# The input loaded already transposed, instead of transposed on TensorE

## The chip, the cores and the metric

The kernel runs on one core of a Trainium2 chip. A core has five engines that work side by side, each in the order of its own instruction stream: TensorE (PE, matrix products), VectorE (DVE), ScalarE (ACT), GpSimd (POOL) and SyncE (SP, which here only issues transfers). They wait for each other by semaphores. Transfers between the main memory and the core's on-chip memory (SBUF) run on 16 DMA engines that all queues share. TensorE reads SBUF and writes PSUM, an accumulator memory of eight banks; DVE and ACT read PSUM back. The metric is the device time of one execution in microseconds (us).

## What is computed

Two attentions over the same input `x` (2048 positions by 640, bf16), with 32 heads of 20 dimensions each, are mixed by a gate. From the reference:

```
g = sigmoid((x * gate_w).sum(-1))
a = A(x, A_wqkv, A_wo)   # softmax(q k^T * 20**-0.5) v for every head, then @ wo
b = B(x, B_wqkv, B_wo)   # each position sees itself and 7 earlier ones, 2 apart
out = g * a + (1 - g) * b
```

A is the costly part: 32 heads by 2048 by 2048 scores, each of which needs an exponential.

## The kernel before, in words

All work is written as tasks by `T(engine, function, reads, writes)`. A planner (`_Sched`) keeps the tasks of an engine in the order in which they are written and derives the semaphore waits from the named buffers. So the order of the source lines is the order on each engine, and SP issues its transfers in that order too.

*The main part.* Heads are taken four at a time (a "quad"), queries 512 at a time. A step computes the scores of two or three pairs (head, block of 128 keys) on PE (line 1241) into PSUM banks 0 to 2 or 3 and 4, and ACT takes the exponential of all of them in one instruction (line 1256). PE multiplies the results with the values (line 1281). 777 such exponentials follow each other. Two fifths of the score blocks go to DVE instead, by an arithmetic exponential (lines 1424 to 1448). The local attention B and the output products are woven between by a list of lanes with due times, planned when the program is built.

*The prologue*, which is all that the change touches, prepares what the first step needs. PE's products contract over the partition dimension, so the input must stand with its 640 features on partitions: `xT[128, 4, 5, 512]`, four stretches of 512 positions, five blocks of 128 features. In order:

- `WqkA` receives the key weights of the first quad by ACT's queue (line 383) and its query weights by SP's (line 388). Between them SP issues eight loads of 256 positions each into `x_tm`, position on partitions (line 385). Behind them on SP come the gate vector `gw` (line 392, 640 single elements) and the value weights `WvA` (line 395).
- `pe_warm` (line 408) issues seven matmuls on zeros while the transfers are on their way.
- `pro_tr(h)` transposes load `h` on PE: ten 128 by 128 blocks, in a group of six and one of four, into PSUM (line 1112). DVE copies the first group to `xT` (line 1124), ACT the second (line 1121).
- `pro_k(h)` computes the keys of the first quad for these 256 positions (five matmuls, line 1136). DVE takes the largest absolute key (line 1140), and ACT then copies the keys to `kT` (line 1142). The transposes and the keys of the eight loads alternate on PE.
- `mk_KM` makes from these maxima a matrix `KM` on DVE (lines 490 and 494), which bounds the scores. `pro_q` computes the first 512 queries (line 1153), DVE takes their absolute value (`q_abs`, line 659), and `q_fin` adds on PE the bound, that is the product of `KM` and that absolute value (line 664), and scales the result on DVE to `qT` (line 667).
- The first three blocks of values (`v_chunk`, 15 matmuls, line 565) are evacuated by ACT (lines 586 and 594). Their weights need the gate vector as a column: a DVE copy into `WvA` (line 1183).
- Two filler matmuls (`pe_fill`, line 1199), and then the first step's scores and its exponential.

On PE the order at the end of the prologue is: the two halves of the first queries, the values, the bound's product, the filler, the first scores. On SP, behind `WvA`, come the key and query weights of the next quads (`ld_wk`, `ld_wq`, line 441, five transfers of 20 KB each, in runs of 40 bytes), the value weights of B (line 674) and, from 48 us on, the other weights of B (`WqkB`, line 888, in runs of 256 bytes).

## Time and profile before

| | us |
|---|---|
| median of 3 runs (894.79 to 896.25) | 895.59 |
| the profiled execution | 894.33 |
| its span in the profile | 892.5 |
| busy: ACT | 876.2 |
| busy: PE | 820.1 |
| busy: DVE | 811.9 |
| busy: POOL | 87.8 |
| first exponential starts at | 18.18 |

The span runs from the first to the last instruction of the profiled execution; what the execution takes beyond it, 1.83 us, lies around it. Times in the views are counted from the span's start. A group of instructions is named by its line, engine and operation, then by what it writes and reads; "idle before" is how long the engine had stood still, and "<-" names what ended that. The profile names a buffer by its memory, so `oTn`, `accW` and `qk` can stand for other buffers that share the place: `accW` in the prologue is the key weights' tile `WkP`.

### The profile page before, as it was taken

Reading aid. Unit: us, or ns where it says so; the run is one execution under the profiler, and the core shown is the slowest. Engines: PE = TensorE matmul, PEld = TensorE weight load, DVE = VectorE, ACT = ScalarE, POOL = GpSimd, SP = SyncE. Lnnn points to the kernel's source line nnn. Section 1 sums busy time; section 2 is a strip of 40 time slices with the busy share of each in tenths; the row PEclk is TensorE's granted clock in tenths of the full one; section 3 lists DMA queues with packets and bytes.
Section 4 is the critical chain, followed back from the end, with each engine's and each line's share of the span. In section 5 each row is a group of like instructions: output and inputs, shape, how many; then the busy total and the mean of one; then the engine's idle time right before and its main releaser. Section 6 shows DMA issues by size and latency. Waiting matters only on the chain.

```text
span 892.5 us, 15877 instructions
## 1 busy us (share of the span) xinstructions
PE 820.1 (92%) x6560; PEld 255.5 (29%) x6560; DVE 811.9 (91%) x1170; ACT 876.2 (98%) x804; POOL 87.8 (10%) x103
## 2 busy tenths in 40 slices
PE   9989999999999998999998889999988999888986
PEld 6322322223323222223332222233222232222322
DVE  6598889999998999999899999999999899999994
ACT  6999999999999999999999999999999999999996
POOL 1000000000000011220002222001322002222000
PEclk9999999999999999999999999999999999999999
DMA  8122101011011456572115658113847003865000
GB/s 181 41 49 48 21 9 10 1 28 7 4 11 14 86 93 94 90 123 37 17 19 88 111 102 145 25 16 56 143 78 108 10 10 74 131 93 89 2 1 30
DMA packets 140988, 51.26 MB, mean 57 GB/s; under 512 B 120436, under 2 KB 128628, under 8 KB 140916
## 3 DMA queue, kind: packets, MB, share of 16 engines
q0 software_dynamic: 13824, 31.46, 20.5%
q1 hardware_dynamic: 126164, 18.35, 13.4%
q8 instruction: 52, 0.85, 0.4%
q10 hardware_dynamic: 928, 0.43, 0.2%
q14 instruction: 20, 0.16, 0.1%
HBM read 16.14 MB, written 2.62 MB: 21 GB/s over the span
## 4 chain that ended last, share of the span: by engine, by line
ACT 94%; PE 2%; DMA 2%; DVE 1%; issue 0%; POOL 0%; DVEq 0%
ACT ebuf L1256 93%; DMA accW<-tmps 1%; PE ps L1112 1%; DMA accW<-xT 1%; PE ps L1136 1%; ACT L_sb L1004 0%; PE ps L411 0%; PE ps L1241 0%; DVE tmps L1069 0%; DVE accW L1059 0%; DVE qk L905 0%; ACT WvB L841 0%; PE ps L565 0%; DVE xH L1436 0%; PE ps L1153 0%
## 5 line engine op out<-in xcount | busy, mean ns | idle before, releaser
L1256 ACT ACTIVATE ebuf<-ps 128x1024 bf16<-128x1024 f32 (+1 forms) x777 | 862.7, 1485 | 0.9 <-PE ps L1241 0.8
L1241 PE MATMUL ps<-qT,kT 32*128 32x512 bf16 x1941 | 305.6, 384 | 63.9 <-ACT ebuf L1256 55.1
L1281 PE MATMUL ps<-ebuf,vA 128*21 128x512 bf16 x1902 | 182.6, 383 | 0.5 <-ACT ebuf L1256 0.5
L1241 PEld LDWEIGHTS ps<-qT,kT 32*128 32x128 bf16 x1941 | 74.3, 91 | 351.7 <-ACT ebuf L1256 327.2
L1424 DVE TENSOR_SCALAR xI<-ps 128x512 int32<-128x512 f32 x146 | 99.4, 686 | 28.3 <-PE ps L1396 14.8
L1436 DVE SCALAR_TENSOR_TENSOR xH<-xU 128x1024 f32<-128x1024 f32 x73 | 88.9, 1218 | 1.4
L1071 POOL DMA_DIRECT2D accW<-tmps x36 | 32.0, 987 | 586.2 <-DVE tmps L1069 545.8
L1439 DVE SCALAR_TENSOR_TENSOR xH<-xH,xU 128x1024 f32<-128x1024 f32 x73 | 88.7, 1216 | 1.0
L1448 DVE SCALAR_TENSOR_TENSOR xo<-xI,xH 128x1024 int16<-128x1024 int32 x73 | 88.7, 1215 | 0.6
L463 PE MATMUL ps<-xT,WqkB 128*128 128x512 bf16 x200 | 59.9, 383 | 0.0
L1281 PEld LDWEIGHTS ps<-ebuf,vA 128*21 128x21 bf16 x1902 | 35.8, 90 | 64.6 <-issue 56.7
L942 DVE TENSOR_TENSOR prod<-qk 128x1024 bf16<-128x1024 bf16 x80 | 51.8, 681 | 0.3 <-PE ps L918 0.3
L1433 DVE TENSOR_SCALAR xU<-xI 128x1024 f32<-128x1024 uint16 x73 | 49.8, 682 | 0.6
L463 PE MATMUL ps<-xT,WqP 128*128 128x512 bf16 x155 | 46.7, 383 | 0.0
L463 PE MATMUL ps<-woA_r,oTn 128*128 128x320 bf16 x236 | 45.3, 301 | 0.0
L463 PE MATMUL ps<-xT,accW 128*128 128x512 bf16 x140 | 42.2, 383 | 0.0
L1717 PE MATMUL ps<-ident,zt 128*128 128x512 bf16 x119 | 40.8, 386 | 0.0
L1712 PE MATMUL ps<-xT,ident 128*128 128x512 bf16 x130 | 40.1, 384 | 0.6 <-DVE qk L905 0.6
L1396 PE MATMUL ps<-qT,kT 32*128 32x512 bf16 x107 | 38.9, 383 | 0.8 <-DVE kT L475 0.7
L1069 DVE TENSOR_TENSOR tmps<-vB,attnT 128x1280 f32<-128x1280 bf16 x24 | 35.5, 1478 | 1.4 <-DMA accW<-tmps 1.4
L1069 DVE TENSOR_TENSOR xT<-vB,attnT 128x1280 f32<-128x1280 bf16 x24 | 35.4, 1477 | 0.3 <-DMA xT<-xT 0.3
L463 PE MATMUL ps<-WvA,oBacc 128*128 128x320 bf16 x160 | 33.2, 302 | 0.1
(122 smaller groups left out, 730.1 us busy)
## 6 DMA issues: line engine op xcount, KB each, us to landing
accW<-tmps POOLq DMA_DIRECT2D x36, 320.0 KB, 4.2
accW<-xT POOLq DMA_DIRECT2D x24, 320.0 KB, 4.0
xT<-xT POOLq DMA_DIRECT2D x24, 320.0 KB, 4.6
WqkB<-in_B_wqkv_dram SPq DMA_DIRECT2D x40, 160.0 KB
xT<-tmps POOLq DMA_DIRECT2D x12, 320.0 KB, 3.8
WqP<-in_A_wqkv_dram SPq DMA_DIRECT2D x135, 20.0 KB
x_tm<-in_A_x_dram SPq DMA_DIRECT2D x8, 320.0 KB
out_dram<-outsb SPq DMA_DIRECT2D x24, 80.0 KB
```

The source lines that it names most:

```text
L463: ins = e.matmul(o, l, r, start=(k0 + k == 0), stop=(k0 + k == n - 1))
L942: t = T("dve", lambda e, r=r, q_ap=q_ap, k_ap=k_ap: e.tensor_tensor(prod[r][:, :, :], q_ap, k_ap, ALU.mult), reads=["qB", "kB"], writes=[( ...
L1069: T("dve", lambda e, vv=vv, av=av, m=m: e.tensor_tensor(tmp4[m], vv, av, ALU.mult), reads=["aT", "vB4"], writes=[("tmps", m)] + dead, cost ...
L1241: ins = e.matmul(bank[b0 + i], kT[32 * j:32 * j + 32, q, kb * P:(kb + 1) * P], qT[gi % NQT][32 * j:32 * j + 32, :], start=True, stop=True)
L1256: return T("act", lambda e: e.activation(ebuf[s % NEB][:, 0:512 * n], ps[:, b0 * 512:(b0 + n) * 512], ACTF.Exp, scale=LN2 / ONE), reads=[( ...
L1281: ins = e.matmul(bank[OB][32 * j:32 * j + DH + 1, :], vA[:, q, kb, VW * j:VW * j + DH + 1], ap, start=st, stop=sp)
L1424: r = T("dve", lambda e, b=b, i=i: e.tensor_scalar(xI[:, 512 * i:512 * i + 512].bitcast(I32), bank[b], XB, 0.0, op0=ALU.add, op1=ALU.max), ...
L1433: T("dve", lambda e: e.tensor_scalar(xU[:, :], xI[:, :].bitcast(U16)[:, 0:2048:2], XV[0], XV[1], op0=ALU.mult, op1=ALU.add), reads=[("xI", ...
L1436: T("dve", lambda e: e.scalar_tensor_tensor(xH[:, :], xU[:, :], XC[0], xU[:, :], ALU.add, ALU.mult), reads=["xU"], writes=["xH"], cost=1220)
L1439: T("dve", lambda e: e.scalar_tensor_tensor(xH[:, :], xH[:, :], XC[1], xU[:, :], ALU.add, ALU.mult), reads=["xU"], writes=["xH"], cost=1220)
L1448: t = T("dve", lambda e, r=r: e.scalar_tensor_tensor(xo[r][:, :].bitcast(I16), xI[:, :].bitcast(I32), XC[2], xH[:, :], ALU.mult, ALU.add), ...
L1717: T("pe", lambda e: e.matmul(bank[OB], zt[:, :], ones4, start=False, stop=False, skip_group_check=True), reads=["ident", "zt"], accum=[("o ...
```

## The change

The eight loads of the input become transposing transfers that write `xT` directly. PE's transposes and the DVE and ACT copies that followed them are left out. The load of the first query weights is issued after the fourth of the eight instead of after the eighth. The keys of the eight loads follow each other on PE. The two halves of the first queries come behind the keys of loads 5 and 6 (counted from 0), and behind the keys of the other six stands a single filler matmul (`pe_idle`). The bound's product, with its scaling to `qT`, is written ahead of the gate vector's copy and of the first values; the values stand directly before the filler. The further weights of the next quad are issued behind the fourth key product in the source, which leaves their place on SP's queue.

```
-        T("sp", lambda e, h=h: e.dma_start(x_tm[:, 2 * h:2 * h + 2, :], x_v[:, 2 * h:2 * h + 2, :]),
-          writes=[("x_tm", h)], dma=True)
-
-    T("sp", lambda e: e.dma_start(WqkA[:, :, 0:80], wA_v[:, :, 0:80]), writes=[("WqA", 0)], dma=True)
+        T("sp", lambda e, h=h: e.dma_start_transpose(xT[:, h // 2, :, 256 * (h % 2):256 * (h % 2) + 256], A_x[0][256 * h:256 * h + 256, :]),
+          writes=[("xTt", h)], dma=True)
+        if h == 3:
+            T("sp", lambda e: e.dma_start(WqkA[:, :, 0:80], wA_v[:, :, 0:80]), writes=[("WqA", 0)], dma=True)
...
+    sch.bufs[("bk", 0)] = [sch.bufs[("bk", 7)][0], []]
...
-    def pro_tr(h):
...
-            T("pe", pe_tr, reads=[("x_tm", h), "ident"], writes=[("bk", b)])
...
-        T("pe", fn, reads=w_keys("WkP", 0) + [("xTt", h, k) for k in range(2)], writes=[("bk", b)], cost=550)
+        T("pe", fn, reads=w_keys("WkP", 0) + [("xTt", h)], writes=[("bk", b)], cost=550)
...
-    pro_tr(0)
-    pro_tr(1)
-    pro_k(0)
...
+    def pe_idle(n):
+
+        def fn(e):
+            ins = None
+            for _ in range(n):
+                ins = e.matmul(bank[0], zt[:, :], fap(zt, zt[:, 0:1], [[0, 4], [1, P]]), start=True, stop=True)
+            return ins
+
+        T("pe", fn, reads=["zt"], accum=[("bk", 0)])
+
+    for h in range(NH):
+        pro_k(h)
+        if h == 3:
             ld_wk(1)
             ld_wq(1)
-    pro_tr(NH - 1)
-    for h in range(NH - 3, NH):
-        pro_k(h)
-        if h == NH - 3:
+        if h == 4:
             mk_q0()
+        if h in (5, 6):
+            pro_q(h - 5)
+        else:
+            pe_idle(1)
     mk_KM(0, 0)
     mk_KM(0, 1)
-    pro_q(0)
+    q_fin(QB0, 0, 0)
     T("dve", lambda e: e.tensor_copy(WvA[:, :, 1:2], gw[:, :].rearrange("p (c k) -> p c k", k=1)), reads=["gw", "WvA"],
       writes=["WvA"], cost=170)
-    pro_q(1)
...
     for i_ in range(3):
         v_chunk(3, 0, 0, i_, i_)
     v_evac(3, 0, 0, "act")
-    q_fin(QB0, 0, 0)
```

30 lines of the change are left out of this document (2 added, 28 removed).

## The prediction

> **What bounds the kernel now.** I read the page's parts 1, 4 and 5 first, to see which engine sets the time.
>
> ```profile
> span 892.5 us, 15877 instructions
> ...
> PE 820.1 (92%) x6560; PEld 255.5 (29%) x6560; DVE 811.9 (91%) x1170; ACT 876.2 (98%) x804; POOL 87.8 (10%) x103
> ...
> ACT 94%; PE 2%; DMA 2%; DVE 1%; issue 0%; POOL 0%; DVEq 0%
> ...
> L1256 ACT ACTIVATE ebuf<-ps 128x1024 bf16<-128x1024 f32 (+1 forms) x777 | 862.7, 1485 | 0.9 <-PE ps L1241 0.8
> ```
>
> The 777 exponentials run on ACT with 0.9 us of idle time in all, 0.8 of it before the first. So the time is the start of the first exponential, a fixed 862.7 us, and the tail. The change lies wholly ahead of the first exponential; what it moves that start by, it moves the end by. The second view is the chain of waits for the first 20 us (start, length, what), which shows what sets that start.
>
> ```profile
> 0.99 3.17 PE ps L411 x7
> 4.16 2.11 PE ps L1112 x20
> ...
> 12.56 1.74 PE ps L1136 x15
> 14.29 1.09 PE ps L1153 x10
> 15.39 0.03 issue
> 15.41 1.23 PE ps L565 x15
> 16.65 0.24 PE ps L664
> 16.89 0.02 issue
> 16.91 0.70 DVE qT L667
> 17.61 0.14 issue
> 17.75 0.41 PE ps L1241 x3
> 18.16 0.02 issue
> 18.18 2.37 ACT ebuf L1256 x2
> ```
>
> PE carries it from 4.16 to 16.89: transposes (L1112), first keys (L1136), first queries (L1153), values (L565), bound's product (L664). The first exponential starts at 18.18. Third, the transfers of the same 20 us, 40 slices of 0.5 us (busy tenths, then rate):
>
> ```profile
> DMA  0005699999999999999999899999623539567747
> GB/s 0 0 0 54 95 323 303 339 397 341 356 374 364 369 364 369 371 361 366 323 198 206 195 310 351 365 235 104 45 12 21 31 21 56 33 38 45 55 30 46
> ```
>
> Summed by slice, 2.73 MB have passed at 10.0 us: the input (2.62 MB, rows of 1280 B) and the 0.10 MB of key weights. The full rate is 366 GB/s, so the input takes 7.16 us. The slow stretch after it holds the query weights and the gate vector; the value weights (WvA, 0.82 MB) end at about 13.45. So the transfers end well before the PE chain needs them. Fourth, the only transfers with the new load's run length: WqkB is read in runs of 256 B, in slices of 0.075 us from 49.5 us.
>
> ```profile
> DMA  7531144889766758999999999999999989642100
> GB/s 44 27 43 27 32 56 96 191 198 236 181 150 140 157 126 181 225 239 277 266 263 253 253 253 287 280 256 277 270 205 229 222 188 201 127 85 48 21 14 17
> ```
>
> With the engines at 9 tenths it holds 253 to 287 GB/s; the middle of the band, less its edges, is about 259.
>
> **The change part by part.**
>
> *Taken out.* PE's 80 transposes (the first 20 matmuls take 2.11 us in the chain, later groups of ten 0.56 each, 5.5 in all), eight DVE copies of 0.55 us, eight ACT copies of 0.59 us. All of it is gone from PE's path. Next late is the DMA.
>
> *The load.* Each of the eight now reads 256 rows by five column blocks, that is 1280 runs of 256 B. No transposing transfer is in this trace. Ends: not under 7.16 us for all eight, the copy rate (the bytes are the same); the slow end is the nearest row of smaller pieces, the key weights' runs of 40 B, at some 36 GB/s from 14 us on: 73 us. I take the row with the same run length, 259 GB/s: 2.621 MB / 259 = 10.12 us, 2.96 more. The ramp at the start (1.5 to 3 us) is kept. So the input ends at 12.96 instead of 10.0, and WvA, which stays behind it on SP's queue, at 16.4 instead of 13.45.
>
> The Trainium skill, "DMA: Bandwidth & Descriptors", § Latency and other measured facts, gives 261 GB/s for a transposing transfer with a non-contiguous middle dimension; by it the load would take 10.04 us and the sum below would be 0.1 us less.
>
> *Issue on SP.* The eight input issues took 0.47 us each; WqkB's 640 runs take 0.37 to issue, so 1280 runs 0.74 us; eight are 5.9 us, under the 10.1 us that the data take: nothing. The other end is WvA, 640 runs in 2.04 us, but those come while its queue is full: 4.1 us for 1280, 33 us for eight. I take 0.74, the row with these runs. The query weights' issue (0.52 us) goes between the fourth and the fifth; the same bytes pass ahead of WvA either way. Later on the queue, the next key weights slip by the same 3 us; they land some 8 us ahead of their first use at 28.3, so nothing.
>
> *The key chain.* From the last load's landing t7 (12.96): product to reduction 0.75 (6.11 to 6.86 in this trace), reduction to the bound KM 0.94 (14.34 to 15.28), bound's product and its scaling to qT 1.13 (16.48 to 17.61), some 0.15 of handovers: qT is there at t7 + 3.0 = 15.96. The first queries' two products and |q| on DVE (0.69) come two loads earlier, between arrivals 1.26 us apart: nothing.
>
> *The bound's product ahead of the values.* The gate column's copy into WvA (0.17, L1183) now stands behind qT on DVE, and the value products wait for that copy. So qT does not overlap the values: with the input free, that order costs. Before, KM's end at 15.28 led to an exponential at 18.18, 2.90. After: 0.05 + 1.13 + 0.05, then 0.22 from copy to values, then 2.0 to the exponential, 3.45. But WvA's landing (16.4) is later than qT (15.96), and so the move costs nothing here. Without WvA's wait it would cost 0.5.
>
> *Values to exponential.* In this trace value products start at 15.41, and ACT has finished their two evacuations at 17.38: 1.97. On PE: 1.07 of values, 0.43 of filler, three score products 0.41 to 0.43: 1.95 to 2.05. Both say 2.0.
>
> *Added.* Six single filler matmuls between keys, about 0.22 us each of issue: in the gaps between arrivals. The one behind the eighth key product lies beside the reduction (0.42): nothing.
>
> *Sum.* 16.4 + 0.05 + 0.22 + 2.0 = 18.67, against 18.18: **+0.5 us**. The profiled execution took 894.33 (span 892.5, 1.83 around it), which gives 894.8; the median shown is 1.26 above the profiled one, so 896.1. The point at which the change turns from gain to loss is an input time of 9.6 us, 272 GB/s: inside the band of WqkB's rates. 0.2% (1.8 us) is about what a measurement of this kernel can tell from no change.
>
> **The rivals.**
>
> *A, the copy rate: faster.* The transposing load keeps 366 GB/s, whatever the runs are, as if whole rows of 1280 B were still fetched. WvA then lands at 13.45 and the exponential starts at 15.72: -2.46, 893.1; at 330 GB/s -1.7, 893.9. For it: the same queue does 366 in this trace. Against it: WqkB's runs never pass 287. It passes 0.2% from 335 GB/s up.
>
> The Trainium skill, "Advanced Engine Details and Errata", § X-Bar Transpose (TRN2), says transposing transfers are as fast as regular ones and expects 350 to 400 GB/s; no run here shows one.
>
> *B, a fixed part in each transposing transfer: slower.* Eight loads stream without a gap before. If each transposing one must drain before the next begins, each pays something of its own start. The nearest row is the ramp, from first bytes at 1.5 to the full rate, worth 1.03 us of full-rate data: seven more of it are 7.2 us, 903.3. It decides from 0.16 us per load (+1.3 on top of the forecast, 897.4). For it: 100 KB of key weights took 3.5 us from issue to landing, though their bytes are worth 0.3 us, so a transfer that must be whole is dear. Against it: nothing here shows that transfers of one queue wait for each other. Its middle is 900.
>
> *C, the PE clock.* The seven warming matmuls of L411 are 0.425 us apart, and filler of the same width later 0.215: half speed until about 4.3 us. The granted clock of the profile reads 1.00 there too, so spacing is what shows it. PE was full after that; now it works some 1.1 of the 3.4 us ahead of the values. If it falls back to half speed there, values and filler take 1.5 us more, the first scores 0.2, and the next 3.3 us, with PE 92% busy, lose 1.3: +3.0, 899.1. Against it: no gap before WvA is longer than some 1.5 us.
>
> The Trainium skill, "TensorE: Matmul & The Clock Gate", § HAM oscillation — how this bites in real kernels, warns of idle gaps over 3.4 us, which by it would leave this kernel at the forecast.
>
> *D, the load broken into small pieces*, each at the price of the key weights' 40 B runs: 73 us instead of 10.1, 959. For it: turning rows into columns scatters what was one run. Against it: nothing in this trace.
>
> The Trainium skill, "VectorE: DVE Perf Modes", § The three transpose paths, gives 1309 ns for one 128 by 128 block by DMA against 390 on TensorE; 80 blocks one after another would by an estimate from that page take 105 us, and no run here shows it.
>
> **How the numbers follow.** Forecast (230 to 290 GB/s, its own range 895.0 to 897.4) 0.32: no change 0.29, slower 0.03. A 0.24: faster 0.21, no change 0.03. B 0.27, C 0.12, D 0.05: slower. So faster 0.21, same 0.32, slower 0.47; the likeliest single case is the forecast, 896.1, though slower has more in sum. The range goes from A's end, 892.9, to B's, 903.5, and leaves out D, B's far part and a little below A, some 0.14.
>
> **What would show it.** In the changed kernel's profile: no L1112 or L1124 rows; input transfers at about 260 GB/s until 13; key products about 1.26 us apart, each waiting for a DMA; the gate copy (L1183's) waiting for WvA's DMA, not for qT; the first exponential near 18.7. A is right if the rate is over 320 and the exponential starts before 16.8; B if the transfers' busy tenths dip between loads; C if the value products (68 ns apart now) are about 134 apart. The forecast is wrong if SP's issues are over 1.3 us each, so that the sequencer paces the load, or if ACT waits between later exponentials by more than now.

## The result, and the profile after

The changed kernel takes 904.7 us in the median of four runs (903.27 to 907.04), against 895.71 for the kernel before beside it (894.79 to 896.25): a ratio of 1.0104, 95% interval 1.0081 to 1.0127. It is slower by 9.0 us. The profiled execution took 903.27, its span 901.4, so 8.9 us more on each than before.

The page of the changed kernel first: span, the shares of the chain, the exponentials.

```profile
span 901.4 us, 15624 instructions
...
ACT 88%; DVE 5%; DMA 3%; SPq 2%; PE 2%; issue 1%; POOL 0%; DVEq 0%
...
L1236 ACT ACTIVATE ebuf<-ps 128x1024 bf16<-128x1024 f32 (+1 forms) x777 | 863.0, 1473 | 2.4 <-PE ps L1221 2.4
```

ACT still sets the time, and its work is the same: 863.0 us against 862.7. Its waits went from 0.9 to 2.4 us, of which 0.7 lies ahead of the first exponential (before: 0.8). (The description of the kernel before gives two fifths of the score blocks to DVE; the page has 146 of the 32 × 16 × 4 = 2048, on line 1424 before and 1404 after, so ACT has 93% of them.) The rest of the 8.9 us is ahead of ACT's main part, in the chain of waits of the first 40 us (start, length, what).

```profile
0.74 1.38 SPq L385
...
13.12 1.84 SPq L385
...
15.00 0.58 SPq L392
...
15.62 5.78 DMA WvA<-in_A_wqkv_dram
...
21.49 0.19 DVE WvA L1165
...
21.73 2.06 PE ps L566 x15
23.79 0.85 PE ps L1179 x2
24.64 0.57 PE ps L1221 x2
...
25.23 15.02 ACT ebuf L1236 x13
```

SP's issues (L385 are the eight input loads) carry the chain until 15.6, then the landing of the value weights, then PE. The first exponential starts at 25.23 instead of 18.18. The accounts, both from profiled executions:

| us | before | after | difference |
|---|---|---|---|
| first exponential starts | 18.18 | 25.23 | +7.05 |
| exponentials, busy | 862.7 | 863.0 | +0.3 |
| waits between later exponentials | 0.1 | 1.7 | +1.6 |
| sum | | | +8.95 (span: +8.9) |

The transfers of the first 20 us, 40 slices of 0.5 us (busy tenths, then rate), answer to the view that the load was priced from:

```profile
DMA  0000999989979967994698999979999793379999
GB/s 0 0 0 15 183 220 266 205 161 113 286 170 179 288 152 154 230 239 83 126 160 172 283 210 183 273 138 109 200 271 182 137 259 8 32 139 284 369 387 366
```

The rate reaches 260 to 290 GB/s again and again and falls to 80 to 150 in between. The input ends at 17.3 instead of 12.96, and the plain copy of WvA behind it runs at 366 to 387. The stretches around the wait for WvA (from:to, length, busy time and count of PE, weight loads, DVE, ACT, POOL, then granted PE clock, DMA share, GB/s):

```profile
20.00:21.00 1.00, 0.00 (x0) 0.00 (x0) 0.20 (x1) 0.00 (x0) 0.00 (x0) 1.00 1.36 108
21.00:22.00 1.00, 0.27 (x4) 0.28 (x5) 0.40 (x2) 0.00 (x0) 0.00 (x0) 0.96 0.47 28
22.00:23.00 1.00, 1.00 (x10) 1.00 (x8) 0.87 (x4) 0.00 (x0) 0.00 (x0) 0.50 0.61 37
```

The clock falls to 0.50 just as the value products begin, and the chain above shows them at 2.06 us, where the chain of before has 1.23. PE had stood from 18.3 to 21.7 but for the bound's product (its weights load at 19.1; the record of its matmul is missing).

So of the 6.56 us by which the first exponential missed the forecast's 18.67, 5.0 are the landing of WvA (21.4 for 16.4) and 1.5 the half clock from the values on.

### The profile page after: what moved, and what is told of

The parts are those of the page before. It is cut to its first block, busy times and chain, and to the rows that moved or that the text cites. A ratio compares the mean times of both kernels' runs of the same rounds, so it can differ in the third digit from the quotient of the medians.

```text
span 901.4 us, 15624 instructions
## 1 busy us (share of the span) xinstructions
PE 803.3 (89%) x6399; PEld 251.3 (28%) x6486; DVE 807.7 (90%) x1162; ACT 872.4 (97%) x796; POOL 87.8 (10%) x103
## 4 chain that ended last, share of the span: by engine, by line
ACT 88%; DVE 5%; DMA 3%; SPq 2%; PE 2%; issue 1%; POOL 0%; DVEq 0%
ACT ebuf L1236 87%; DMA xT<-xT 1%; SPq L385 1%; DVE prod L943 1%; DVE xT L1070 1%; DMA WvA<-in_A_wqkv_dram 1%; DVE xo L1428 1%; DMA accW<-tmps 1%; DVE xI L1404 0%; PE ps L1221 0%; ACT L_sb L1005 0%; PE ps L1692 0%; DVE xH L1419 0%; PE ps L1261 0%; DVE xH L1416 0%
## 5 line engine op out<-in xcount | busy, mean ns | idle before, releaser
L1236 ACT ACTIVATE ebuf<-ps 128x1024 bf16<-128x1024 f32 (+1 forms) x777 | 863.0, 1473 | 2.4 <-PE ps L1221 2.4
L464 PE MATMUL ps<-xT,WqkB 128*128 128x512 bf16 x179 | 53.3, 383 | 1.8 <-issue 1.6
L464 PE MATMUL ps<-xT,WqP 128*128 128x512 bf16 x136 | 41.5, 383 | 1.5 <-issue 1.1
L464 PE MATMUL ps<-xT,accW 128*128 128x512 bf16 x126 | 38.1, 383 | 1.6 <-issue 1.4
L1692 PE MATMUL ps<-xT,ident 128*128 128x512 bf16 x113 | 35.8, 387 | 3.9 <-DVE xI L1404 1.8
L566 PE MATMUL ps<-WvA,xT 128*128 128x160 bf16 (+1 forms) x320 | 31.0, 238 | 3.5 <-DVE WvA L1165 3.5
```

The source lines that it names most:

```text
L464: ins = e.matmul(o, l, r, start=(k0 + k == 0), stop=(k0 + k == n - 1))
L1236: return T("act", lambda e: e.activation(ebuf[s % NEB][:, 0:512 * n], ps[:, b0 * 512:(b0 + n) * 512], ACTF.Exp, scale=LN2 / ONE), reads=[( ...
```

## The experiments

Three questions were open. First, why the load is slow: "issue" says that SP's sequencer paces it, "stream" that the transposing transfers are slow in the DMA engines and SP only waits for room; later "runs" blames the 256 B runs, "mixing" the plain transfers among transposing ones, "boundary" the change from one transposing transfer to the next, "size" the small piece. Second, whether the late start passes to the end. Third, what the half clock and the new order cost. The kernel before took 895.3 to 895.7 in the median beside each of them.

**probe_sizes.** The transfers alone, each waited for before the next, then groups back to back.

```
+ e.dma_start_transpose(xT[:, 0, :, :], x[0:256, :])   # waited for; then other shapes
+ for h in range(8): e.dma_start_transpose(xT[:, h, :, :], x[256*h:256*h+256, :])
...
+ for c in range(5): e.dma_start(xR[:, :, :, c, :], x_v[:, :, c*P:(c+1)*P])   # runs of 256 B
```

> A program of transfers alone, all issued from SP; it leaves out the whole computation, and what it writes out is the input. First, transposing loads one at a time, each waited for before the next is issued (256 by 640 twice, 128 by 640, 64 by 640, 512 by 640, 1024 by 640, 256 by 256, 256 by 128, 128 by 128), then one plain load of 256 by 640 and one of its first 128 columns; then eight transposing loads of 256 by 640 back to back, four of 512 by 640, eight plain ones, and the same bytes in runs of 256 B. Theory 'issue' (SP makes the pieces of a transposing load one by one, and this paces the eight): with the queue empty the 256 by 640 load still takes 1.4 to 1.8 us to issue, the 512 one twice that, the 128 one half; back to back the eight take 8 x 1.7 = 13.6 us, the four the same in all. Theory 'stream' (the data path of the transposing loads is slow, and the issue only waits for room in the queue): alone, issue takes 0.4 to 0.7 us whatever the size, and only the later ones of a row of eight take 1.7. Theory 'fixed part' (my rival B): the time from issue to landing is nearly the same for all sizes, and four of 512 rows take half as long as eight of 256. Plain loads: eight in 7.2 us at 366 GB/s; in runs of 256 B 10.1 us at 259.

SP's time, in order (start, length until SP went on, what): single loads of 256, 512 and 1024 rows; then eight transposing, four transposing of 512 rows, eight plain, five plain in runs of 256 B.

```profile
0.73 1.32 SPq L36 DMA_TRANSPOSE xT<-in_A_x_dram  x1
...
12.96 2.66 SPq L40 DMA_TRANSPOSE xQ<-in_A_x_dram  x1
17.66 4.87 SPq L41 DMA_TRANSPOSE t<-in_A_x_dram  x1
...
36.97 13.51 SPq L50 DMA_TRANSPOSE xT<-in_A_x_dram  x8
52.82 12.69 SPq L56 DMA_TRANSPOSE xQ<-in_A_x_dram  x4
67.72 4.21 SPq L62 DMA_DIRECT2D xN<-in_A_x_dram  x8
77.92 9.26 SPq L68 DMA_DIRECT2D xR<-in_A_x_dram  x5
```

A single transposing issue costs SP 1.3 us for 256 rows, and the load lands 3.5 us after it began. The next issue's start shows the whole: 4.70 us for 512 rows (12.96 to 17.66), 6.99 for 1024, so 512 rows more cost 2.29 us, 286 GB/s. Eight back to back hold SP 13.5 us, 1.69 each, and take 15.85 to the last landing; eight plain loads take 10.2, the same bytes in runs of 256 B 14.1 (7.2 and 10.1 were said). Four of 512 rows take 14.9, not half of the eight, so "fixed part" as it was put falls. So the disputed cost is there without a kernel around it, and a long transposing transfer is no slower than the 259 GB/s of the forecast. Neither theory fits the single issues: "issue" had 1.4 to 1.8 us for 256 rows and half of it for 128, "stream" 0.4 to 0.7 whatever the size, and they took 1.32 for 256 rows, 1.20 for 128 and 2.66 for 512. The probe does not tell whether SP or the engines pace the eight.

**aux_on_act.** All plain loads of the prologue on ACT's queue, so that only the eight are left on SP.

```
-        if h == 3:
-            T("sp", lambda e: e.dma_start(WqkA[:, :, 0:80], ...
+    T("act", lambda e: e.dma_start(WqkA[:, :, 0:80], ...
...
-    T("sp", sp_gw, ...); T("sp", lambda e: e.dma_start(WvA[...
+    T("act", sp_gw, ...); T("act", lambda e: e.dma_start(WvA[...
```

> The changed kernel with the query weights, the gate vector and the value weights issued on ACT's queue at the start, so that they do not stand behind the eight transposing loads. Theory 'issue': the DMA engines have room beside the eight, so the last lands 0.6 us earlier (the query weights' issue is gone) at about 16.6, the value weights by 9; the bound is ready as before relative to it, the scaling ends at 19.6, the first exponential starts at 22 with the clock up and 23.5 with PE at half speed: 1.7 to 3.2 us less than the changed kernel's 25.23. Theory 'stream': 0.92 MB more share the engines with the eight, the last lands 2.5 us or more later, about 19.5, the first exponential starts at 24.5 to 25.5: no gain.

```profile
0.74 19.56 SPq L385 DMA_TRANSPOSE xT<-in_A_x_dram  x8
```

Measured: 905.68 (904.62 to 907.43), ratio 1.0112 [1.0095, 1.0129]. The eight issues took 19.56 us instead of 13.5, the last load landed at 22.64, and the first exponential started at 29.20 in the profiled execution, which was the slowest of the four (907.43). The issues got longer although nothing was put on SP, so it was not SP's own work that stretched them, and the earlier landing that "issue" forecast did not come. Whether SP paces an undisturbed row of eight this run can't tell; probe_cuts, below, has more on it. "Stream" had the direction, but its 24.5 to 25.5 is too early: the last landing came 5.3 us later than in the changed kernel, where 0.92 MB at 366 GB/s are 2.5 us, so the plain transfers beside the transposing ones cost more here than their bytes explain.

**plain256.** The changed kernel with sixteen plain loads whose runs are 256 B. Its `xT` holds other values than the transposed input.

```
-        T("sp", lambda e, h=h: e.dma_start_transpose(xT[...], A_x[0][256 * h:256 * h + 256, :]),
+        for i in range(2):
+            T("sp", lambda e, h=h, i=i: e.dma_start(xT[:, h // 2, :, 256 * (h % 2) + P * i:256 * (h % 2) + P * i + P],
+                                                    x_v[:, 2 * h + i, :].rearrange("p (c k) -> p c k", c=CN)),
```

> [...] In the program of transfers alone, the whole input in runs of 256 B took 14.1 us from the first issue to the last landing, 15.9 transposed, 10.2 plain. Theory 'runs' (most of what the transposing loads cost is that they read 256 B at a time, not the transposition): the value weights land some 4 us later than in runs of 512 B, at 17.5, and the first exponential starts at 20 to 21.5; the transposition is left with about 2 to 4 of the 7 us. Theory 'transposition' (the run length is harmless at 259 GB/s, as I forecast): value weights at 16.4, the first exponential at 18.7, the changed kernel's other 6.5 us belong to the transposition.

Runs of 256 B settled at some 218 GB/s without dips (the transfers from 9 us on, 200 to 228 in slices of 0.35 us), WvA landed at about 18.2, the first exponential started at 21.43, and the time was 900.41 (899.44 to 904.82), 1.0058 [1.0036, 1.008]. So even the price of short runs, which the forecast took from WqkB at 259, was 218 on this queue. The start lies where "runs" put it (20 to 21.5): plain runs of 256 B in this order cost 3.3 of the change's 7.05 us, and 3.8 are left for the transposition and the half clock that came with its later landing. The gate copy (19.16) waited for `qT` last, not for WvA.

**plain512.** The same with eight loads in runs of 512 B (two rows on one partition).

```
+        T("sp", lambda e, h=h: e.dma_start(xT[:, h // 2, :, 256 * (h % 2):256 * (h % 2) + 256],
+                 A_x[0][256 * h:256 * h + 256, :].rearrange("(p i) d -> p (i d)", i=2).rearrange("p (c k) -> p c k", c=CN)),
```

> The changed kernel with its eight transposing loads replaced by eight plain ones of the same bytes into the same places, two adjacent rows to a partition, in runs of 512 B. The input is then not transposed, so what is computed from it is not the reference's result; all instructions and waits behind the loads are the same. It gives what the rest of the change is worth if the load costs what a plain one does (my rival A). My account: input at about 10 us, value weights at 13.5, first exponential at 15.7 with the clock up, 17.2 with PE at half speed; the whole 2.5 us faster than the kernel before, 1 us if at half speed. Rival: the order behind the loads costs so much that even then the kernel is no faster (first exponential at 18 or later).

Measured: some 270 to 310 GB/s from 8 us on, WvA landed at 16.68 instead of 13.5, the values ran at half clock (1.65 us), first exponential 20.11; 898.42 (895.86 to 900.05, ten runs), 1.0028 [1.0017, 1.004]. Runs of 512 B don't reach the copy rate either. This kernel is the nearest to what the forecast described, a load without gaps, with WvA 0.3 us from its place (16.4): the exponential came 1.4 later than forecast all the same, the values and what follows at half clock.

**hybrid2.** The kernel before, its last two input loads transposing.

```
+        if h >= 6:
+            T("sp", lambda e, h=h: e.dma_start_transpose(xT[:, h // 2, :, 256 * (h % 2):256 * (h % 2) + 256], ...
+            continue
...
     def pro_tr(h):
+        if h >= 6:
+            return
```

> The kernel before, with only the last two of its eight input loads turned into transposing ones; the other six are transposed on PE, and the order behind is that of the kernel before. My account: PE's chain loses two of its eight transposes (1.1 us) and DMA gains two times 0.8 us, so that the value weights land at about 15.1, just as the bound is ready (14.2): the first exponential starts 0.3 to 1.0 us earlier, at 17.2 to 17.9, a gain of about 0.05 to 0.1%, hardly to be told in the time. Rival: the two transposing loads and the gate vector's single elements slow each other, the value weights land after 16.5, and the kernel is 1 us or more slower.

SP's time on the six plain and the two transposing issues:

```profile
0.74 3.01 SPq L389 DMA_DIRECT2D x_tm<-in_A_x_dram  x6
3.80 6.64 SPq L386 DMA_TRANSPOSE xT<-in_A_x_dram  x2
```

Six plain issues took 0.50 us each, the two behind them 4.03 and 2.56, against 1.32 in an empty queue; what they waited for the trace does not show. WvA landed at 17.94 instead of the 15.1 that was said, the first exponential started at 21.04 instead of 17.2 to 17.9, time 898.59 (896.34 to 900.7, twelve runs), 1.0031 [1.002, 1.0042]. With two transposing loads the start is already 2.9 us later.

**probe_mix.** Transfers alone again, groups each waited for in full.

```
+ for h in range(6): plain(h)
+ for h in range(6, 8): tr(h)
...
+ for h in range(4): tr(h)
+ e.dma_start(wq, wA_v[:, :, 0:80])      # query weights
+ for h in range(4, 8): tr(h)
```

> A second program of transfers alone, all from SP; it leaves out the whole computation, and what it writes out is the input. Groups, each waited for in full before the next: the input plain in runs of 1280, 512 and 256 B; eight transposing loads; one transposing load of all 2048 rows; six plain then two transposing; two transposing then six plain; four transposing, the query weights, four transposing; query weights, gate vector and value weights alone; eight transposing, gate vector, value weights; runs of 256 B again. Theory 'runs and transposition': from first issue to last landing 10, 11.5, 14, 16 us for the first four; the one load of everything about 12 (a fixed 2.4 and 9.2 at the 286 GB/s between the sizes of 512 and 1024 rows). Theory 'mixing' (a transposing load and a plain one in the same queue hold each other up; in the kernel with two transposing loads these took 6.6 us to issue): six plain and two transposing take over 13 us where their parts' shares of the pure groups sum to some 11.5; the query weights amid the eight cost 1 us or more over the pure eight plus their own 0.5. Rival: mixed groups cost what their parts do.

| group | us, first issue to last landing |
|---|---|
| eight plain | 11.0 |
| eight transposing | 15.6 |
| one transposing load of all 2048 rows | 11.53 |
| six plain, two transposing | 11.86 |
| two transposing, six plain | 12.45 |
| four transposing, query weights, four transposing | 16.56 |
| eight transposing, gate vector, value weights | 20.24 |

"Mixing" falls for these groups: six plain and two transposing take 0.3 us more than one transposing load, where over 13 was said. The query weights in the middle cost 1.0 us, not nothing, and that group's 16.56 is what the changed kernel's input took, 17.32 − 0.74 = 16.58. The two groups meant for short runs wrote neighbouring places and were joined into longer pieces, so they measured nothing about runs. The row that matters is the third: the same bytes, the same kind of transfer, but one instruction instead of eight, and 4.1 us less.

**probe_cuts.** The same 2048 rows, transposing, cut in different ways.

```
+ for h in range(8):  e.dma_start_transpose(big[:, :, 256*h:256*h+256], x[256*h:256*h+256, :])
+ e.dma_start_transpose(big[:, :, :], x[:, :])
+ for h in range(2):  ... 1024 rows    for h in range(4): ... 512 rows    for h in range(16): ... 128 rows
+ for c in range(5):  e.dma_start_transpose(big[:, c, :], x[:, 128*c:128*c+128])
```

> A third program of transfers alone (no computation; it writes out the input): all 2048 rows transposed into one place, cut differently: eight loads of 256 rows, one of 2048, two of 1024, four of 512, sixteen of 128, five of 128 columns each, one of 1792 and one of 256 rows, eight again, two again. So far one took 11.5 us from issue to landing, four 14.9, eight 15.6 to 15.9. Theory 'boundary' (each start of a transposing load behind another costs): two take 12.1 to 12.6, sixteen 19 to 20, five columns 14 to 16, and the rate dips once per boundary. Theory 'size' (only loads of many rows reach the full rate): two take 11.6 like one, five column loads of all rows 11.6 too, sixteen more than 20.

SP's time, in order: eight loads, one, two, four, sixteen, five of 128 columns.

```profile
0.73 13.25 SPq L51 DMA_TRANSPOSE big<-in_A_x_dram  x8
16.65 9.46 SPq L54 DMA_TRANSPOSE big<-in_A_x_dram  x1
28.28 10.50 SPq L58 DMA_TRANSPOSE big<-in_A_x_dram  x2
40.94 12.37 SPq L62 DMA_TRANSPOSE big<-in_A_x_dram  x4
55.43 21.00 SPq L66 DMA_TRANSPOSE big<-in_A_x_dram  x16
78.16 12.93 SPq L70 DMA_TRANSPOSE big<-in_A_x_dram  x5
```

Each group begins when the one before has landed, so the differences of the starts are the whole times: 15.92, 11.63, 12.66, 14.49, 22.73; five took 15.06, to the start of a group not shown. The transfers of the one load, slices of 0.29 us:

```profile
GB/s 0 0 0 0 27 122 105 220 231 276 287 289 291 291 287 294 289 286 293 291 291 286 294 289 291 289 294 288 287 293 291 289 289 291 292 286 293 149 4 0
```

And of the four, slices of 0.36 us:

```profile
GB/s 0 0 0 34 191 117 209 268 291 290 290 156 116 146 56 111 291 290 290 291 192 113 90 155 268 284 292 289 269 79 81 168 143 244 268 290 290 259 24 0
```

One load runs flat at 290 GB/s; four run at the same 290 with three dips to 56 to 156, each at a boundary. Per boundary: (12.66 − 11.63) / 1 = 1.0 us for two loads, 0.95 for four, 0.86 for five, 0.6 for eight, 0.74 for sixteen; a load of 1792 rows and one of 256, also run, took 12.22, 0.6. "Boundary" holds, though sixteen were to take 19 to 20 and took 22.7. "Size" falls: two and five loads are large and pay as much at each boundary. SP's own work per issue explains little of it: the issues of eight, four and two loads, at what each took in an empty queue (1.32, 2.66, 4.87 us), add up to 10.6, 10.6 and 9.7 us, against 9.46 for one load; back to back they held SP for 13.25, 12.37 and 10.50. So of 3.8, 2.9 and 1.0 us more, at most 1.1, 1.2 and 0.3 are such work; the rest does not show in an empty queue. Why a boundary costs this is not shown; the traces show that the engines' rate falls there, not what they wait for.

**four_loads.** The use of that: four transposing loads of 512 rows, with the query weights on ACT's queue ahead and the fillers of clock_fill and wq_first, below.

```
-        T("sp", lambda e, h=h: e.dma_start_transpose(xT[...256 wide...], A_x[0][256 * h:256 * h + 256, :]),
+        if h % 2 == 0:
+            T("sp", lambda e, h=h: e.dma_start_transpose(xT[:, h // 2, :, :], A_x[0][256 * h:256 * h + 512, :]),
```

> The changed kernel with the query weights on ACT and the fillers that keep the clock up (the run wq_first), with four transposing loads of 512 rows instead of eight of 256; the key products start in pairs. Theory 'boundary': four boundaries fewer are worth 0.7 to 1.0 us in the transfers alone, so the value weights land at 20.3 instead of 21.2 and the whole is about 0.8 us faster than wq_first (901.19), which the spread of the runs may hide. Rival: no gain, since the first keys come later and the pairs cost 0.8 us behind the last landing.

Two lines of the chain of waits:

```profile
6.82 1.25 PE ps L1113 x5
8.06 1.71 PE ps L1146 x4
```

The fast part of WvA's copy ended at about 18.7 instead of 20.0 in the changed kernel (read from the rates), but PE, idle until 6.82, ran the first keys and the added fillers at half clock (1.25 us for the five key products, 0.72 at full clock in the changed kernel), and its chain reached 19.2. `KM` was there at 20.7, the gate copy was done at 22.0, and the ten added fillers then held PE until 23.2; the first exponential came at 25.20: 902.72 (901.24 to 906.56), 1.0083 [1.0062, 1.0104]. The gain of the load was given back by PE. A kernel with one or two transposing loads, the cuts that cost least alone, was not run.

**late_wva.** The kernel before, with a plain copy of the input's size put ahead of the gate vector: WvA late without any transposition.

```
+    T("sp", lambda e: e.dma_start(kT[:, 1:6, :]..., x_v), writes=[("kT", q, t) for q in range(1, 6) for t in range(4)], dma=True)
     def sp_gw(e):
```

> The kernel before, with a plain load of 2.62 MB of input into an unused stretch put on SP's queue between the query weights and the gate vector: the value weights land 7.2 us later, at 20.6, and everything else stays. It takes away the transposing loads and keeps their delay. My account: the values start at 20.9; PE has idled for over 3 us by then and runs at half speed, so the first exponential starts 3.5 us later at 24.4 (22.9 with the clock up), and the end moves by the same 6.2 us, and by a further 1 to 2 us if later exponentials wait more because of the shift, as in the changed kernel (+1.6). Rival: only the transposing loads do that to the later part; here the end moves by exactly what the start moves.

```profile
11.90 10.13 DMA WvA<-in_A_wqkv_dram
...
22.36 2.21 PE ps L568 x15
...
26.30 3.71 ACT ebuf L1259 x3
```

In its chain of waits WvA lands at 22.0 (20.6 was said), the values run at half clock (2.21), the first exponential starts at 26.30 (24.4 was said), 8.12 later than before. The time is 903.57 (903.36 to 904.55), 1.0095 [1.008, 1.011], 8.3 more than the kernel before beside it. In the profiled execution the span is 901.7, 9.2 more: the 8.1 of the start, and 1.0 of waits between later exponentials at 808 to 814 us, where the clock fell again. So the delay of the start passes to the end in full, the later waits come on top, as the first account and not the rival had it, and neither they nor the half clock need a transposing transfer.

**clock_fill.** The changed kernel, with more filler work for PE between the keys and ahead of the values.

```
-            pe_idle(1)
+            pe_idle(4)
...
     q_fin(QB0, 0, 0)
+    pe_idle(10)
```

> The changed kernel with more filler on PE: four instead of one behind each of six key products, and ten between the bound's product and the first values, so that PE has work while it waits for the loads. My account: the clock stays up; the values and the filler take 1.5 us where they took 2.9, the first exponential starts at 23.7 if the value weights land at 21.4 as before, and the whole is 1.5 us faster than the changed kernel, or 2 with fewer waits later. Rival: the fillers themselves come late (PE is still busy with them when the value weights land), no gain.

```profile
16.19 6.07 DMA WvA<-in_A_wqkv_dram
...
22.58 1.23 PE ps L566 x15
...
24.62 6.05 ACT ebuf L1237 x5
```

In this chain the values take 1.23 us instead of 2.06, and the first exponential starts 2.04 us after the values do instead of 3.50. WvA happened to land 0.9 later, so the start gained 0.6. The time is 901.54 (900.71 to 903.57), 1.0058 [1.0041, 1.0075]: 3.2 us better than the changed kernel in the medians. The profiled execution, 903.57, is the slowest of its four and no shorter than the changed kernel's (903.27), though its first exponential is 0.6 earlier: the clock fell after 800 us here too, with 2.0 us of waits. So the half clock is shown as a cost of about 1.5 us ahead of the first exponential; the rest of the 3.2 is not placed.

**wq_first.** clock_fill, with the query weights issued on ACT ahead of everything.

```
+    T("act", lambda e: e.dma_start(WqkA[:, :, 0:80], wA_v[:, :, 0:80]), writes=[("WqA", 0)], dma=True)
     for h in range(NH):
...
-        if h == 3:
-            T("sp", lambda e: e.dma_start(WqkA[:, :, 0:80], ...
```

> The changed kernel with the fillers of the run above that kept the clock up, and with the query weights issued from ACT at the start, behind the key weights, so that no plain load stands between the transposing ones. Theory 'mixing': the gap between the fourth and the fifth landing (2.9 us where others are 1.3 to 1.9) closes, the value weights land 1.2 us earlier at 21.0, the first exponential starts at 23.4 instead of 24.62, the whole is about 1 us faster than with the fillers alone (901.54). Rival: the 0.10 MB cost the same 0.3 to 0.5 us wherever they stand: no gain.

Measured: the gate copy started at 21.17 instead of 22.35, the first exponential at 23.44 instead of 24.62, both 1.2 earlier as said. The median, 901.19 (899.31 to 902.97), 1.0061 [1.0042, 1.0079], doesn't show it; four runs each don't resolve 1 us here.

**order_alone.** The kernel before with the second part of the change only: the bound's product ahead of the first values.

```
     pro_q(0)
+    pro_q(1)
+    q_fin(QB0, 0, 0)
     T("dve", lambda e: e.tensor_copy(WvA[:, :, 1:2], ...
...
     v_evac(3, 0, 0, "act")
-    q_fin(QB0, 0, 0)
```

> The kernel before with the second part of the change alone: the bound's product and its scaling stand ahead of the gate vector's copy and of the first values; loads and transposes are those of before, and the two halves of the first queries stand directly ahead of it. My account: the product waits for the absolute queries on DVE (16.1), then product and scaling to 17.45, the copy to 17.6, and only then the values, so the first exponential starts at 19.6 instead of 18.18: 1.5 us slower. Rival: scaling and values overlap and it is as fast or up to 0.5 us faster.

```profile
17.75 0.18 DVE WvA L1185
...
17.97 1.23 PE ps L565 x15
...
20.00 10.57 ACT ebuf L1256 x9
```

The gate copy waits behind `qT` and starts at 17.75, the values at 17.97 instead of 15.41, the first exponential at 20.00, 1.8 later. Time 897.47 (896.19 to 898.39, ten runs), 1.0024 [1.0014, 1.0033], 1.9 us (1.5 was said). Of the 1.8 in the profile, 0.5 is there already when `KM` is ready (15.81 instead of 15.28; the first load landed later), and the order costs the other 1.3: from `KM` to the exponential 4.19 us instead of 2.90. Here the queries' absolute value (0.69 us on DVE) also stands behind `KM`, which it doesn't in the changed kernel. Where WvA is in time, this order costs.

**order_undone.** The changed kernel with that order taken back.

```
-    q_fin(QB0, 0, 0)
     T("dve", lambda e: e.tensor_copy(WvA[:, :, 1:2], ...
...
     v_evac(3, 0, 0, "act")
+    q_fin(QB0, 0, 0)
```

> The changed kernel with the bound's product put back behind the first values, where it stood before; the transposing loads stay. The values start when the value weights land (21.4), as in the changed kernel; behind them the product and its scaling (1.1 us with a warm clock, 1.3 without) come before the scores. My account: the first exponential starts about 0.8 to 1.2 us later than 25.23, and the whole takes that much longer. Rival: the product's place makes no difference (within 0.3 us), since the values' evacuation on ACT ends last.

```profile
22.31 1.23 PE ps L566 x15
23.54 0.24 PE ps L665
23.80 0.70 DVE qT L668
...
25.08 5.97 ACT ebuf L1236 x5
```

In this chain `qT` (23.80) follows the values instead of lying under the wait for WvA: from WvA's landing at 21.98 to the first exponential 3.10 us. With the new order it is 2.36 at full clock (clock_fill) and 3.83 at half (the changed kernel). By these profiles the new order is worth some 0.7 us when WvA is late and the clock is up, and in the changed kernel the half clock outweighed it. The first exponential came at 25.08, not 0.8 to 1.2 later than 25.23 as was said; the clock stood at 1.00 when the values began, though PE had waited 3.0 us without a break. The times are the same, 904.7 (901.86 to 905.85), 1.0101 [1.0079, 1.0122]: nothing of it can be told in the median.

**plain2560 and plain2560b.** What the rest of the change is worth if the load had the copy rate: plain loads in runs of 2560 B into `xT` (which then holds other values), so that a key product has to wait for two of them. plain2560 also has one filler more behind the keys and three behind the bound's product; plain2560b has the change's own.

```
-        T("sp", lambda e, h=h: e.dma_start_transpose(xT[...], A_x[0][256 * h:256 * h + 256, :]),
+        T("sp", lambda e, h=h: e.dma_start(xT[:, h // 2, :, :]...[:, 1280 * (h % 2):1280 * (h % 2) + 1280],
+                                           A_x[0][256 * h:256 * h + 256, :].rearrange("(p i) d -> p (i d)", i=2)),
-        T("pe", fn, reads=w_keys("WkP", 0) + [("xTt", h)], ...
+        T("pe", fn, reads=w_keys("WkP", 0) + [("xTt", 2 * t), ("xTt", 2 * t + 1)], ...
```

> The changed kernel with plain loads in runs of 2560 B (two adjacent rows to a partition, one stretch), so that the load costs what it does in the kernel before; each key product waits for its pair of loads. The input is not transposed, so what is computed is not the reference's result. Two fillers instead of one behind the keys and three behind the bound's product. My account: the input at 10.1 us, value weights at 13.5, the first exponential at 15.8, the whole 2.4 us (0.27%) faster than the kernel before: the rest of the change is then worth what my rival A said. Rival: as in the run with 512 B, the value weights land late all the same, since two queues' worth of small pieces pass ahead of them, and the kernel is no faster.

> The run plain2560 with the changed kernel's own fillers (one behind six of the keys, none behind the bound's product): there my two and three fillers had kept PE busy until 13.3, so that PE and not the loads set the start. The input is not transposed, the result not the reference's. My account of rival A: the input at 10.1, keys to 11.9, the bound at 12.9, scaling to 14.0, value weights at 13.5, the first exponential at 16.4: 1.8 us (0.2%) faster than the kernel before, less what later exponentials wait after a drop of the clock (1 to 2 us in runs where it drops). Rival: the first exponential is no earlier than 17.5, and the change could not have gained even with loads at the plain price.

The loads ran mostly at 350 to 420 GB/s. plain2560: 896.42 (894.12 to 897.86, eleven runs), 1.0009 [1.0001, 1.0018], first exponential 17.68 (15.8 was said); its added fillers kept PE busy until 13.3 and so set the start. plain2560b: 896.79 (894.64 to 900.02, twelve runs), 1.0011 [0.9998, 1.0023]; its chain of waits:

```profile
13.52 0.69 DVE qabs L661
14.22 0.34 DVE Kmax L1118
...
14.78 0.29 DVE KM L496
...
...
16.39 1.23 PE ps L567 x15
...
18.42 12.83 ACT ebuf L1237 x11
```

The exponential was to start at 16.4 and started at 18.42. The first keys ran at half clock (1.23 us), the absolute value of the queries (0.69) stood on DVE ahead of the last reduction, and from KM's end at 15.07 to the exponential it took 3.35 us. So without a slow load the change gains nothing in this form. That the keys wait in pairs is the test's own, so how much a real load at that rate would have gained stays open.

**The starts and the times together.** For each kernel of the whole computation, how much later its first exponential starts than before's 18.18 (one profile), and its median less 895.5 (the kernels before beside them had 895.3 to 895.7):

| kernel | start later by | median longer by |
|---|---|---|
| plain2560 | −0.5 | 0.9 |
| plain2560b | 0.2 | 1.3 |
| order_alone | 1.8 | 2.0 |
| plain512 | 1.9 | 2.9 |
| hybrid2 | 2.9 | 3.1 |
| plain256 | 3.3 | 4.9 |
| wq_first | 5.3 | 5.7 |
| clock_fill | 6.4 | 6.0 |
| order_undone | 6.9 | 9.2 |
| four_loads | 7.0 | 7.2 |
| the change | 7.1 | 9.2 |
| late_wva | 8.1 | 8.1 |
| aux_on_act | 11.0 | 10.2 |

The two columns agree within 2.3 us, although the kernels differ in all else. In the profiled executions, where start and span belong to the same run, the span is longer by the shift of the start and a rest. The rest is −0.1 to 0.7 us in the four kernels in whose profile the clock stays at 1.00 after 800 us (order_alone, order_undone, wq_first, plain2560), and 1.1 to 3.1 us in the nine in which it falls there. None of these versions beats the kernel before.

## Why the prediction was wrong, step by step

**What bounds the kernel: right.** ACT's 777 exponentials and their start set the time. The change moved the start by 7.05 us and the span by 8.9; late_wva moved the start by 8.1 and the span by 9.2 with another cause. But "what it moves that start by, it moves the end by" left something out: the forecast had nothing for the 1.6 us of waits between later exponentials, which it had named as a sign of being wrong.

**"The load" and "Issue on SP": here the prediction failed.** The price for bytes in motion was not the error: a single transposing load runs at 290 GB/s, better than the 259 taken, and past the break-even of 272. The step that failed is the term of 10.12 us for the input, in its assumption that eight loads stream without a gap. They don't: cut into eight, the same bytes take 4.1 us more (15.6 against 11.53), some 0.6 for each of seven boundaries. That is rival B's mechanism, inside its bounds of 0.16 to 1.03 per load and given 0.27 (the 0.16 takes eight loads for its 1.3 us; over seven boundaries it is 0.19). What a boundary waits for stays open. The sign that it named is there: the busy tenths dip between loads. In the miss of 5.0 us for WvA's landing the terms are: the rate −0.7 (a single load issued at 0.74 would have ended at 12.3 instead of 12.96), the boundaries +4.1, the query weights in the middle +1.0 (taken as nothing), and the gate vector with WvA 4.1 instead of 3.45, +0.65. They sum to +5.0.

The issue on SP, taken as 0.74 us, was 1.38 to 1.84, past the 1.3 us that the prediction named as the sign that the sequencer paces the load. The sign misleads: alone, an issue takes 1.3, but among others it takes longer (19.56 us for eight in aux_on_act, 4.03 for one behind plain loads in hybrid2). What it takes beyond 1.3 does not show in an empty queue; that it waits for room there is the likeliest reading, and not shown.

The Trainium skill, "DMA: Bandwidth & Descriptors", § Latency and other measured facts, puts a transposing transfer with a non-contiguous middle dimension at 261 GB/s; the runs show 290 for one load, and about 190 for eight of them in a row, from the first bytes to the last, so neither end is that figure. The Trainium skill, "Advanced Engine Details and Errata", § X-Bar Transpose (TRN2), expects 350 to 400; no transposing transfer here passed some 294.

**"The key chain": right.** From the last load's landing (17.32) to `qT` (20.20) 2.9 us, forecast 3.0.

**"The bound's product ahead of the values": right in its condition, and near in its size.** It costs where WvA is in time: in plain2560b KM's end to the exponential took 3.35 (forecast 3.45, before 2.90). order_alone's 1.9 us say nothing on the 0.5 that was forecast, since its queries come later than the change's. In the changed kernel WvA lands after `qT`, as forecast, and the order costs nothing; against the other order it gains some 0.7 at full clock, by one profile of each.

**"Values to exponential": right at full clock, wrong in the event.** 2.0 was forecast; clock_fill measured 2.04, the changed kernel 3.50, because the clock fell (rival C, given 0.12, priced +1.7 for this piece). The argument against it was that no gap before WvA would be longer than 1.5 us. With WvA 5 us late, PE stood 3.5 us, with only the bound's product in it. plain512 shows it with WvA only 0.3 us behind the forecast, so C was likelier than 0.12 even at the forecast's own rate. Here it came with B: a late load lengthens the wait in which the clock can fall (it did here and in late_wva, not in order_undone), so they should not have been priced as cases apart. The two together still end inside the range: 895.7 and the start's 7.05 make 902.8. It took the 1.6 us of later waits and 0.3 of longer exponentials on top to pass its end, 904.7 against 903.5.

The Trainium skill, "TensorE: Matmul & The Clock Gate", § HAM oscillation — how this bites in real kernels, ties the fall to idle gaps of over 3.4 us. Here the longest unbroken gap was about 2.2 us, behind a product at 19.1 to 19.5, and the clock fell all the same; in order_undone PE stood for 3.0 us without a break and the clock stayed at 1.00, and in aux_on_act it fell at 25.9 with no gap over 0.9 us in the 6 us before. So the length of the gap does not settle it in these runs, and what does is open.

**Rival C's later part, and the 1.6 us.** C had 1.3 us for later score products at half clock, in the wrong place. In the changed kernel the loss is not in the 3.3 us behind the first scores but late, and only in part of this kind. Stretches of the changed kernel, columns as above:

```profile
803.00:807.00 4.00, 2.96 (x36) 0.73 (x24) 3.86 (x5) 4.00 (x5) 0.58 (x1) 1.00 0.90 164
807.00:810.00 3.00, 2.67 (x15) 0.61 (x14) 3.00 (x4) 2.68 (x3) 0.00 (x0) 0.50 0.02 5
```

The clock falls to 0.50 behind a stretch in which PE worked 2.96 of 4.00 us. What ACT waits for then, by the order of time on ACT (start, length from first to last, what, idle before):

```profile
809.30 1.02 ACT L1236 ACTIVATE ebuf<-ps 128x1024 bf16<-128x1024 f32 x1 [0.32 <-PE ps L1221]
810.97 11.40 ACT L1236 ACTIVATE ebuf<-ps 128x1536 bf16<-128x1536 f32 x10 [0.64 <-PE ps L1221]
```

Those are 0.96 of the 1.7 us. The other 0.7 ends at 703.0 us, at a clock of 1.00: there PE, which works in its own order, had waited 1.22 us for DVE's line 1404 before it came to the scores. A thin stretch alone doesn't bring the fall: before had 2.96 of 4.00 too, from 796 to 800, at a clock of 1.00. A late fall stands in the profiles of nine kernels, this one among them, but not in those of the kernel before, order_alone, order_undone, wq_first and plain2560. What decides whether it comes is open; it was not tried by itself.

**Rival A: not reached.** A transposing load never had the copy rate, and plain2560b shows that even a plain load at that rate gained nothing in this order and with PE at half clock for the first keys. **Rival D: nothing of it**; the load takes 16 us, not 73.

## What to carry to other kernels

A rate taken from bytes in motion prices one transfer; a row of transfers of a new kind also needs a price for each boundary, and if no trace has one, the case "each pays its own start" deserves the larger chance. When a wait gets longer, ask in the same breath what the waiting engine's clock does meanwhile, and add the two rather than weigh them as alternatives. And when the removed work ran beside a transfer that was early (PE's transposes here), count as gained only what lies between that transfer's end and the end of the work, not the work.

## What the runs showed that was not expected

- A transposing load of this shape runs at 290 GB/s, and cutting it costs 0.6 to 1.0 us at each cut: 11.6 us for one instruction, 12.7 for two, 14.5 to 14.9 for four, 15.6 to 15.9 for eight, 22.7 for sixteen.
- Plain loads differ by run length: 366 GB/s for 1280 B, mostly 350 to 420 for 2560 B, some 270 to 310 for 512 B, some 218 for 256 B; the transposing load, whose runs are 256 B, is above the plain one of the same runs.
- Transposing transfers beside plain ones from another queue came down to rates of 40 to 75 GB/s in all (aux_on_act, 5.25 to 7.5 us), while six plain and two transposing alone on one queue took no more than 11.9 us; what makes the difference was not found.
- The kernel before's own runs spread from 894.1 to 897.5, and the spread goes with the granted clock: 0.998 to 1.0 in every run under 895.1, 0.996 in all but one above 896.5.
